# Linear attention ahead of two MoE layers: the low part of each turned chunk moves from VectorE to GpSimd, the squares are folded once, the scale goes into omega, and chunk 0 is prepared ahead of the loop

## The chip, the cores and the metric

The kernel runs on one core of a Trainium2 chip. The metric is the device time of one launch in microseconds. The engines are named as in the profile: PE is TensorE, ACT is ScalarE, DVE is VectorE, POOL is GpSimd, and SP is the engine whose queue issues the DMAs.

## The reference

Three stages run one behind the other, all in float32. Only the first is touched by the change.

```python
def _attn_ref(q, k, v, omega):            # q, k, v: (4, 8, 576, 64), omega: (128, 64)
    scale = 1.0 / np.sqrt(np.sqrt(D))
    q_s, k_s = (q * scale, k * scale)
    def phi(x):
        proj = np.einsum('bhsd,md->bhsm', x, omega)
        sq = np.sum(x * x, axis=-1, keepdims=True) / 2.0
        h = proj - sq
        h = h - np.max(h, axis=-1, keepdims=True)
        return np.exp(h) / np.sqrt(m)
    q_p, k_p = (phi(q_s), phi(k_s))
    kv = np.einsum('bhsm,bhsd->bhmd', k_p, v)
    z = np.sum(k_p, axis=2)
    num = np.einsum('bhsm,bhmd->bhsd', q_p, kv)
    den = np.einsum('bhsm,bhm->bhs', q_p, z)[..., None] + 1e-06
    return num / den
```

Behind it come a gated feed-forward layer (2304 tokens, 512 to 1536 to 512) and a second layer of 8 experts with a gate that is balanced by 8 rounds of row and column sums.

## The kernel before

Matmuls keep float32 precision by splitting each operand into a high part (a rounded copy, made by ACT) and a low part (the operand less the high part), and adding three products: high by high, high by low, low by high. For a chunk of the attention these are lines L529, L530 and L531; L531 is the one that reads the low part of the chunk.

The attention cuts q and k into 36 chunks of 128 partitions by 512 columns: a tail of k, then k and q in turn, with the tails of k and q in between. From chunk 1 on the odd chunks are k and the even ones q, but for the tails (17 is a tail of k, 18 and 35 are tails of q). Each chunk is loaded twice, turned (`xt`) for the matmul and as it is (`x`) for the sum of squares.

The work is a software pipeline that is written out by hand. A loop runs over steps; in each step the list `ORDER` is gone through from first to last, and an entry `(name, k)` does stage `name` for chunk `step - k`. Each engine does its instructions in the order in which they are written, so `ORDER` fixes every engine's queue. The stages that matter here, with the lines of the profile:

- `s0` (one chunk ahead, k = -1): POOL squares `x` (L492) into the one buffer `xx`, folds 64 columns to 32 (L494) and 32 to 16 (L495).
- `s0r` (k = 0): DVE sums the rest to `ssq` (L501). `s0n` (k = 0): POOL scales it to `nsq` (L507).
- `s1a` (k = 1): ACT makes the high part of the turned chunk (L477). `s1b` (k = 1): DVE makes its low part (L481).
- `s2p` (k = 2): PE projects the chunk, 12 matmuls (L529 to L531). `s2m`: DVE takes the maxima of both halves (L536). `s2b`, `s2c`: DVE makes `hm` (L540) and the bias `bi` (L544). `s2x`: ACT does the exponentials with that bias (L551, 8 instructions).
- `s3` to `s5` (k = 3 to 8): sums of keys by values (L566, L567) for a k chunk; transposes, numerator, division and the way back (L571, L584, L600, L612 to L622, L632, L643, L648) for a q chunk. On ACT two of these stand ahead of `s1a` in every even step, the copy L584 and the cast L643; in odd steps there is none.
- `pump`: twice in a step, one piece of the conversion of the next layer's float64 weights (L195 to L213 and L181), on ACT, DVE or POOL.

In ACT's queue the cast of chunk n (`s1a`, in step n + 1) stands behind the exponentials of chunk n - 2 (step n). From the last steps on the first MoE layer fills PE, which stays full to the end of the kernel. The chunk `x` has three buffers and the turned one four.

Of the kernel before, what the change touches and what calls it, by code (L numbers as in the profile page):

```python
# [11 lines left out]
F32 = mybir.dt.float32  # L12
F32R = mybir.dt.float32r
AF = mybir.ActivationFunctionType
ALU = mybir.AluOpType
# [5 lines left out]
P = 128  # L21
# [13 lines left out]
SCALE = float(D) ** -0.25  # L35
# [11 lines left out]
def f(ap):  # L47
    return ap.bitcast(F32)


class Kernel:
    def __init__(self, tc, x, v, vt, omega, wg, wv, wo, w2g, w1, w2, out):
# [7 lines left out]

    ORDER = [("s3a0", 4), ("s0r", 0), ("s5a", 8), ("s2p0", 2), ("s1a", 1), ("s2m0", 2), ("s2p1", 2), ("s40", 5),
# [3 lines left out]
    RINGS = dict(tr3=(0, 3), tr5=(4, 5, 6, 7, 2, 1), pr=(4, 5, 6, 7, 2, 1), nu=(4, 5, 6,  # L67
                 7, 2, 1), a=(0, 1, 2, 3), b=(4, 5, 6, 7))

# [329 lines left out]
    def attention(self, m1):  # L399
        tc, nc = self.tc, self.nc  # L400
        if True:
# [8 lines left out]
            sm = af  # L410
# [6 lines left out]
            om2 = t3[:, 0, 0:M]  # L417
            bdh, bdl = t6[:, 0], t6[:, 1]
# [19 lines left out]
            NCH = len(chunks)  # L438
            st = [dict() for _ in chunks]
# [4 lines left out]
            def load(i):  # L444
                side, bp, hp, j = chunks[i]
                c = st[i]
                n = 8 if hp is None else 2 * hp + j
                k = turn("x", 3)
                xt = c["xt"] = xts[turn("xt", 4)]
                c["x"] = t0[:, k].rearrange("p (a d) -> p a d", d=D)  # L450
                for w, t in ((1, xt), (0, t0[:, k])):
                    nc.sync.dma_start(t, self.x["qk".index(side), w, bp, n])
                c["idx"] = (lambda a, h: 2 * a + h) if hp is None else (lambda a, h: 4 * h + a)

            def loadv(i):
                side, bp, hp, j = chunks[i]
                c = st[i]
                if side == "q":
                    return
                if hp is None:  # L460
                    c["vz"] = vzts[2 * bp:2 * bp + 2]
                    for j in range(2):
                        nc.sync.dma_start(c["vz"][j].rearrange("p a d -> p (a d)"), self.vt[bp, j])
                else:
                    z = c["vz"] = vz[nvz[0] % NVZ]
                    nvz[0] += 1
                    nc.sync.dma_start(z.rearrange("p a d -> p (a d)"), self.v[bp, 2 * hp + j])
# [10 lines left out]

            def s1b(i):
                c = st[i]  # L480
                nc.vector.tensor_tensor(c["xl"], c["tr"], f(c["xh"]), op=ALU.subtract)  # L481

            def s0(i):
                c = st[i]
                sqv = c["x"]
                if i < self.EARLY:
                    c["xx"] = t2[:, i].rearrange("p (a d) -> p a d", d=D)
                    c["ssq"] = sm.tile([P, 8], F32, tag="ssq", name=f"ssq{i}", bufs=4)
                    nc.scalar.activation(c["xx"], sqv, AF.Square)
                    return  # L490
                xx = t0[:, 3].rearrange("p (a d) -> p a d", d=D)
                nc.gpsimd.tensor_tensor(xx, sqv, sqv, op=ALU.mult)  # L492
                ssq = sm.tile([P, 8], F32, tag="ssq", name=f"ssq{i}", bufs=4)
                nc.gpsimd.tensor_tensor(xx[:, :, 0:32], xx[:, :, 0:32], xx[:, :, 32:64], op=ALU.add)  # L494
                nc.gpsimd.tensor_tensor(xx[:, :, 0:16], xx[:, :, 0:16], xx[:, :, 16:32], op=ALU.add)  # L495
                c["xx"], c["ssq"] = xx, ssq

            def s0r(i):
                c = st[i]
                xx = c["xx"] if i < self.EARLY else c["xx"][:, :, 0:16]  # L500
                nc.vector.tensor_reduce(c["ssq"], xx, axis=AX.X, op=ALU.add)  # L501

            def s0n(i):
                c = st[i]
                nsq = sm.tile([P, 8], F32, tag="nsq", name=f"nsq{i}", bufs=4)
                eng = nc.vector if i < self.EARLY else nc.gpsimd
                eng.tensor_scalar(nsq, c["ssq"], -SCALE * SCALE / 2, None, op0=ALU.mult)  # L507
                c["nsq"] = nsq

            def s2(i):  # L510
                side, bp, hp, j = chunks[i]
# [25 lines left out]

            def s2b(i):
                c = st[i]
                nc.vector.scalar_tensor_tensor(c["hm"], c["mx"], SCALE, c["nsq"], op0=ALU.mult, op1=ALU.add)  # L540

            def s2c(i):
                c = st[i]
                nc.vector.scalar_tensor_tensor(c["bi"], c["hm"], -1.0, c["nsq"], op0=ALU.mult, op1=ALU.add)  # L544

            def s2x(i, u):
                c = st[i]
                e, bi = c["e"], c["bi"]
                for a in range(4 * u, 4 * u + 4):
                    pr = c["pr"][a // 4].rearrange("p w (h m) -> p (w h) m", m=M)  # L550
                    nc.scalar.activation(e[:, a, :], pr[:, a % 4, :], AF.Exp, bias=bi[:, a:a + 1], scale=SCALE)  # L551

            def s3(i, h):
                side, bp, hp, j = chunks[i]
# [94 lines left out]
                st[i] = None  # L649

            pump = lambda i: self.attn_pump()
            fns = dict(s0=s0, s0r=s0r, s0n=s0n, s1=s1, s1a=s1a, s1b=s1b, s2=s2, s2b=s2b, s2c=s2c, s4r=s4r, s5=s5, s5a=s5a, s5b=s5b, pump=pump)
            halves = dict(s2p=s2p, s2m=s2m, s2x=s2x, s3=s3, s3a=s3a, s4=s4, s4d=s4d, s4n=s4n)

            def stage(n):
                if n in fns:
                    return fns[n]
                g, h = halves[n[:-1]], int(n[-1])
                return lambda i: g(i, h)

            order = [(stage(n), k) for n, k in self.ORDER]
            nc.sync.dma_start(om2, self.omega)
            load(0)
            load(1)
            for h in range(2):
                r = slice(h * D, (h + 1) * D)
                nc.scalar.copy(bdh[r, h, :], om2[r])
                nc.vector.tensor_tensor(bdl[r, h, :], om2[r], f(bdh[r, h, :]), op=ALU.subtract)
            s0(0)
            for step in range(NCH + 8):  # L670
                if step == NCH + 2:
                    self.rings = self.DRAIN
                if step + 2 < NCH:
                    load(step + 2)
                if step == 0:
                    loadv(0)
                if step + 1 < NCH:
                    loadv(step + 1)
                for fn, n in order:
                    i = step - n  # L680
                    if 0 <= i < NCH:
                        fn(i)
                self.attn_hook(step)
                if step >= NCH + 2:
                    next(m1)
# [868 lines left out]
```

## Time and profile before

| | |
|---|---|
| time, median of 3 runs | 2113.62 us (2111.9 to 2114.81) |
| span of the profiled execution | 2111.6 us; its own time is not listed apart |
| PE busy over the span | 2061.5 us (98%) |
| DVE, POOL, ACT busy over the span | 66%, 50%, 39% |

The span runs from the first to the last instruction; what the median has over it (2.0 us) lies around it. Busy shares are over the whole span, and the attention is only about its first 180 us, so the stretch of the attention has to be looked at by itself.

### The profile page before, as it was taken

What the parts mean: (1) busy time and instruction counts of PE and PEld (TensorE: products, weight loads), DVE (VectorE), ACT (ScalarE), POOL (GpSimd) and SP (SyncE); (2) the same over time, 40 slices, a digit from 0 to 9 for tenths busy, and PEclk for the clock granted to TensorE, in tenths of its full rate; (3) what the DMA queues carried; (4) which work ended last, traced back from release to release, by engine and by line L of the source; (5) the groups of instructions that cost most, each with busy time, mean ns of one, the idle gap of its engine ahead of it and who ended that gap; (6) DMA issues with size and microseconds to landing.
All of it is one profiled execution on the core that took longest, in us unless ns stands there. A gap on an engine that the chain in (4) does not pass through costs nothing.

```text
span 2111.6 us, 32611 instructions
## 1 busy us (share of the span) xinstructions
PE 2061.5 (98%) x11836; PEld 1991.5 (94%) x11836; DVE 1400.0 (66%) x2321; ACT 825.3 (39%) x1843; POOL 1053.2 (50%) x1047
## 2 busy tenths in 40 slices
PE   7999999999999999999999999999999999999998
PEld 6889999999998889998898999999999999999998
DVE  6996678778655645444544666666687666666666
ACT  6776433333335444433433432323323432323322
POOL 6783656656533455545642544343454444343443
PEclk9999999999999999999999999999999999999999
DMA  6452556555424665666668777777877877787884
GB/s 212 166 165 66 176 165 200 179 165 187 133 80 175 235 236 209 253 254 251 230 254 301 242 259 257 260 255 263 278 259 268 273 258 258 258 257 255 244 269 152
DMA packets 238129, 467.76 MB, mean 222 GB/s; under 512 B 20272, under 2 KB 110096, under 8 KB 233872
## 3 DMA queue, kind: packets, MB, share of 16 engines
q1 hardware_dynamic: 237968, 465.68, 65.7%
q8 instruction: 93, 1.52, 0.3%
q14 instruction: 68, 0.56, 0.1%
HBM read 340.25 MB, written 125.35 MB: 220 GB/s over the span
## 4 chain that ended last, share of the span: by engine, by line
PE 89%; DVE 7%; POOL 1%; issue 1%; DMA 1%; ACT 1%; SPq 0%; DVEq 0%; ACTq 0%; POOLq 0%
PE bank L1079 12%; PE pair L1416 7%; PE pair L1418 7%; PE pair L1417 7%; PE bank L1325 7%; PE bank L1327 7%; PE bank L1326 7%; PE bank L723 5%; PE bank L724 5%; PE bank L725 5%; PE bank L1020 4%; PE bank L1022 3%; PE bank L1021 3%; PE bank L755 2%; PE bank L757 2%; PE bank L756 2%
## 5 line engine op out<-in xcount | busy, mean ns | idle before, releaser
L1428 DVE TENSOR_TENSOR sums<-pair,sums 128x768 f32<-128x768 f32 x209 | 198.7, 951 | 44.4 <-PE pair L1418 44.3
L1325 PE MATMUL bank<-xh,ar 128*128 128x384 f32 x564 | 188.7, 335 | 2.4 <-ACT mt L1358 2.0
L1327 PE MATMUL bank<-xh,ar 128*128 128x384 f32 x564 | 188.5, 334 | 0.0
L1326 PE MATMUL bank<-xl,ar 128*128 128x384 f32 x564 | 188.4, 334 | 0.0
L1095 DVE SCALAR_TENSOR_TENSOR ac<-bank,mt,ac 128x512 f32<-128x512 f32 x84 | 63.0, 750 | 129.9 <-PE bank L1079 128.1
L1416 PE MATMUL pair<-xh,ar 128*128 128x384 f32 x344 | 115.3, 335 | 0.0
L1417 PE MATMUL pair<-xl,ar 128*128 128x384 f32 x344 | 114.9, 334 | 0.0
L1418 PE MATMUL pair<-xh,ar 128*128 128x384 f32 x344 | 114.9, 334 | 0.0
L1325 PEld LDWEIGHTS bank<-xh,ar 128*128 128x128 f32 x564 | 105.9, 188 | 3.4 <-ACT mt L1358 2.7
L1326 PEld LDWEIGHTS bank<-xl,ar 128*128 128x128 f32 x564 | 105.9, 188 | 0.0
L1327 PEld LDWEIGHTS bank<-xh,ar 128*128 128x128 f32 x564 | 105.9, 188 | 0.0
L737 ACT CAST ar<-mt 128x384 fp32r<-128x384 f32 x72 | 37.0, 514 | 171.9 <-DVE mt L734 171.9
L723 PE MATMUL bank<-xh,ar 128*128 128x384 f32 x288 | 96.7, 336 | 0.0
L725 PE MATMUL bank<-xh,ar 128*128 128x384 f32 x288 | 96.2, 334 | 0.0
L725 PE MATMUL bank<-xh,ar1b 128*128 128x384 f32 x288 | 96.2, 334 | 0.0
L724 PE MATMUL bank<-xl,ar 128*128 128x384 f32 x288 | 96.2, 334 | 0.0
L724 PE MATMUL bank<-xl,ar1b 128*128 128x384 f32 x288 | 96.2, 334 | 0.0
L723 PE MATMUL bank<-xh,ar1b 128*128 128x384 f32 x288 | 96.2, 334 | 0.0
L551 ACT ACTIVATE at<-bank,bi 128x128 f32<-128x128 f32 x288 | 78.2, 383 | 42.5 <-DVE bi L544 33.2
L1020 PE MATMUL bank<-xh,ar 128*128 128x384 f32 x264 | 89.4, 338 | 3.2 <-DVE st L1054 2.5
L1022 PE MATMUL bank<-xh,ar 128*128 128x384 f32 x264 | 88.7, 336 | 2.8 <-DVE ar L265 2.7
L1021 PE MATMUL bank<-xl,ar 128*128 128x384 f32 x264 | 88.3, 335 | 0.0
(382 smaller groups left out, 6919.9 us busy)
## 6 DMA issues: line engine op xcount, KB each, us to landing
ar<-w2forms SPq DMA_DIRECT2D x144, 512.0 KB, 4.5
ar<-w1forms SPq DMA_DIRECT2D x141, 512.0 KB, 4.9
ar1b<-w1forms SPq DMA_DIRECT2D x62, 512.0 KB, 4.9
ar1b<-w2forms SPq DMA_DIRECT2D x61, 512.0 KB, 4.5
w2forms<-ar SPq DMA_DIRECT2D x224, 128.0 KB, 4.1
w1forms<-ar SPq DMA_DIRECT2D x22, 1280.0 KB, 7.1
sumsraw<-in_w_dram SPq DMA_DIRECT2D x32, 512.0 KB, 4.5
w2forms<-sumsraw SPq DMA_DIRECT2D x128, 128.0 KB, 2.7
```

What stands on the lines that cost most here:

```text
L723: nc.tensor.matmul(t, hi[:, c, fs], self.xh[:, c, cs], start=(c == 0), stop=False)
L724: nc.tensor.matmul(t, hi[:, c, fs], self.xl[:, c, cs], start=False, stop=False)
L725: nc.tensor.matmul(t, lo[:, c, fs], self.xh[:, c, cs], start=False, stop=(c == KC - 1))
L1020: nc.tensor.matmul(g, ah[:, c, :], bh[:, c, :], start=(first and c == 0), stop=False, skip_group_check=not first)
L1079: nc.tensor.matmul(y, a, w[:, fi % 2, ds], start=(first and x == 0 and k == 0 and fi == fis[0]), stop=(last and x == 1 and fi == fis[-1]))
L1325: nc.tensor.matmul(g, w[:, 0, d], bh[:, d, :], start=bool(first and d == 0), stop=False, skip_group_check=not first)
L1326: nc.tensor.matmul(g, w[:, 0, d], bl[:, d, :], start=False, stop=False, skip_group_check=not first)
L1327: nc.tensor.matmul(g, w[:, 1, d], bh[:, d, :], start=False, stop=(d == 1), skip_group_check=not first)
L1416: nc.tensor.matmul(y, w[:, k, 0, ds], h, start=(k == 0), stop=False)
L1417: nc.tensor.matmul(y, w[:, k, 0, ds], l, start=False, stop=False)
L1418: nc.tensor.matmul(y, w[:, k, 1, ds], h, start=False, stop=(k == 1))
L1428: v.tensor_tensor(a[n], pair, a[n], op=ALU.add)
```

## The change

The low part of a chunk (`s1b`) goes from DVE to POOL for every chunk but chunk 0, and its entry in `ORDER` moves up to stand right behind `s1a`, ahead of `s0`. `s0` loses its second fold, so `s0r` reads 32 columns in place of 16. `s0n` is gone: `hm` and `bi` are each made in one step from `ssq`. The scale is put into omega once, ahead of the loop. `s1`, `s1a`, `s1b` and `s0` of chunk 0 (`EARLY` is 1) are done ahead of the loop.

```diff
-    ORDER = [("s3a0", 4), ("s0r", 0), ("s5a", 8), ("s2p0", 2), ("s1a", 1), ("s2m0", 2), ("s2p1", 2), ("s40", 5),
-             ("s2m1", 2), ("s2b", 2), ("s2c", 2), ("s3a1", 4), ("s0", -1), ("s1b", 1), ("pump", 3), ("s2", 1),
+    ORDER = [("s3a0", 4), ("s0r", 0), ("s5a", 8), ("s2p0", 2), ("s1a", 1), ("s1b", 1), ("s2m0", 2), ("s2p1", 2),
+             ("s40", 5), ("s2m1", 2), ("s2b", 2), ("s2c", 2), ("s3a1", 4), ("s0", -1), ("pump", 3), ("s2", 1),
...
             def s1b(i):
                 c = st[i]
-                nc.vector.tensor_tensor(c["xl"], c["tr"], f(c["xh"]), op=ALU.subtract)
+                eng = nc.vector if i < self.EARLY else nc.gpsimd
+                eng.tensor_tensor(c["xl"], c["tr"], f(c["xh"]), op=ALU.subtract)
...
                 nc.gpsimd.tensor_tensor(xx[:, :, 0:32], xx[:, :, 0:32], xx[:, :, 32:64], op=ALU.add)
-                nc.gpsimd.tensor_tensor(xx[:, :, 0:16], xx[:, :, 0:16], xx[:, :, 16:32], op=ALU.add)
...
-                xx = c["xx"] if i < self.EARLY else c["xx"][:, :, 0:16]
+                xx = c["xx"] if i < self.EARLY else c["xx"][:, :, 0:32]
                 nc.vector.tensor_reduce(c["ssq"], xx, axis=AX.X, op=ALU.add)
-
-            def s0n(i):
...
-                nc.vector.scalar_tensor_tensor(c["hm"], c["mx"], SCALE, c["nsq"], op0=ALU.mult, op1=ALU.add)
+                nc.vector.scalar_tensor_tensor(c["hm"], c["ssq"], -SCALE * SCALE / 2, c["mx"], op0=ALU.mult, op1=ALU.add)
...
-                nc.vector.scalar_tensor_tensor(c["bi"], c["hm"], -1.0, c["nsq"], op0=ALU.mult, op1=ALU.add)
+                nc.vector.scalar_tensor_tensor(c["bi"], c["ssq"], -SCALE * SCALE / 2, c["hm"], op0=ALU.mult, op1=ALU.subtract)
...
-                    nc.scalar.activation(e[:, a, :], pr[:, a % 4, :], AF.Exp, bias=bi[:, a:a + 1], scale=SCALE)
+                    nc.scalar.activation(e[:, a, :], pr[:, a % 4, :], AF.Exp, bias=bi[:, a:a + 1])
...
-                nc.scalar.copy(bdh[r, h, :], om2[r])
-                nc.vector.tensor_tensor(bdl[r, h, :], om2[r], f(bdh[r, h, :]), op=ALU.subtract)
-            s0(0)
+                nc.scalar.activation(bdh[r, h, :], om2[r], AF.Copy, scale=SCALE)
+                nc.vector.scalar_tensor_tensor(bdl[r, h, :], om2[r], SCALE, f(bdh[r, h, :]), op0=ALU.mult, op1=ALU.subtract)
+            for fn in (s1, s1a, s1b, s0):
+                for i in range(self.EARLY):
+                    fn(i)
...
-                    if 0 <= i < NCH:
+                    if 0 <= i < NCH and not (i < self.EARLY and fn in (s1, s1a, s1b, s0)):
                         fn(i)
```

The line numbers of the changed kernel are a few lower (L481 becomes L482, L492 L493, L494 L495, L540 L533, L544 L537). On POOL, in the middle of the attention, one step stood like this before (`at_96` holds `x` and the squares; L210 and L213 are pieces of the weight conversion):

```order
L210 TENSOR_TENSOR m1raw_0_1_183<-m1raw_0_1_183 128x512
L492 TENSOR_TENSOR at_96<-at_96 128x512
L494 TENSOR_TENSOR at_96<-at_96 128x8x32
L495 TENSOR_TENSOR at_96<-at_96 128x8x16
L507 TENSOR_SCALAR nsq_733<-ssq_644 128x8
L213 TENSOR_TENSOR cv<-cv,m1raw_0_1_183 128x512
```

The same place in the changed kernel (`ar_62` holds the high and low parts of the turned chunks):

```order
L210 TENSOR_TENSOR m1raw_0_1_174<-m1raw_0_1_174 128x512
L482 TENSOR_TENSOR ar_62<-turned,ar_62 128x512
L493 TENSOR_TENSOR at_96<-at_96 128x512
L495 TENSOR_TENSOR at_96<-at_96 128x8x32
L213 TENSOR_TENSOR cv<-cv,m1raw_0_1_174 128x512
```

The low part now stands in POOL's queue ahead of the squares of the chunk two further on, and the second fold and `nsq` are gone. On DVE one step stood like this before:

```order
L501 TENSOR_REDUCE ssq_297<-at_96 128x8
L536 TENSOR_REDUCE mx_302<-bank_79 128x4
L536 TENSOR_REDUCE mx_302<-bank_71 128x4
L540 SCALAR_TENSOR_TENSOR hm_303<-mx_302,nsq_268 128x8
L544 SCALAR_TENSOR_TENSOR bi_304<-hm_303,nsq_268 128x8
L481 TENSOR_TENSOR ar_62<-turned,ar_62 128x512
L206 TENSOR_SCALAR m1raw_0_0_181<-cv 128x512
```

The same step on DVE in the changed kernel:

```order
L501 TENSOR_REDUCE ssq_283<-at_96 128x8
L529 TENSOR_REDUCE mx_286<-bank_79 128x4
L529 TENSOR_REDUCE mx_286<-bank_71 128x4
L533 SCALAR_TENSOR_TENSOR hm_287<-ssq_198,mx_286 128x8
L537 SCALAR_TENSOR_TENSOR bi_288<-ssq_198,hm_287 128x8
L206 TENSOR_SCALAR m1raw_0_0_172<-cv 128x512
```

The low part is gone from DVE's queue; the sum L501 still stands ahead of the two maxima. The order on ACT and on PE is the same in the loop.

## Rows read from the trace of the kernel before

**Rows 1.** The page: busy time, share of the span and instructions of each engine.

```profile
PE 2061.5 (98%) x11836; PEld 1991.5 (94%) x11836; DVE 1400.0 (66%) x2321; ACT 825.3 (39%) x1843; POOL 1053.2 (50%) x1047
```

**Rows 2.** Busy us (instructions) of each engine by stage, clock, DMA share, GB/s.

```profile
43.80:165.90 122.10, 112.09 (x934) 106.89 (x932) 116.19 (x261) 95.52 (x294) 92.99 (x118) 0.97 0.50 164
180.00:200.00 20.00, 20.00 (x150) 19.62 (x150) 13.14 (x26) 8.85 (x19) 9.60 (x11) 1.00 0.08 25
```

**Rows 3.** The chain that ended last, 100 to 110: start, us, what.

```profile
105.49 1.23 DVE ar L481
...
106.77 0.38 PE bank L531
```

**Rows 4.** Groups by line, 43.8 to 165.9: busy us, mean ns, idle before.

```profile
L481 DVE TENSOR_TENSOR ar<-turned,ar 128x512 fp32r<-128x512 f32 x27 | 26.6, 985 | 0.0
L492 POOL TENSOR_TENSOR at<-at 128x512 f32<-128x512 f32 x25 | 26.0, 1039 | 20.0 <-DVE ssq L501 19.9
L507 POOL TENSOR_SCALAR nsq<-ssq 128x8 f32<-128x8 f32 x27 | 16.5, 610 | 3.0 <-DVE ssq L501 0.8
L495 POOL TENSOR_TENSOR at<-at 128x128 f32<-128x128 f32 x26 | 14.1, 542 | 2.0
L181 POOL TENSOR_TENSOR ar<-cv,ar 128x512 fp32r<-128x512 f32 x5 | 6.4, 1288 | 0.4
L206 DVE TENSOR_SCALAR m1raw<-cv 128x512 int32<-128x512 int32 x5 | 2.1, 416 | 0.0
```

**Rows 5.** DVE's timeline, steps 21 and 22: start us, us, what.

```profile
98.31 0.27 DVE L501 TENSOR_REDUCE ssq<-at 128x8 f32<-128x128 f32 x1
...
99.81 0.72 DVE L540 SCALAR_TENSOR_TENSOR hm<-mx,nsq 128x8 f32<-128x8 f32 x1
100.56 0.17 DVE L544 SCALAR_TENSOR_TENSOR bi<-hm,nsq 128x8 f32<-128x8 f32 x1
100.64 0.96 DVE L481 TENSOR_TENSOR ar<-turned,ar 128x512 fp32r<-128x512 f32 x1
```

**Rows 6.** POOL's timeline there.

```profile
98.66 1.04 POOL L492 TENSOR_TENSOR at<-at 128x512 f32<-128x512 f32 x1 [1.44 <-DVE ssq L501]
99.78 0.72 POOL L494 TENSOR_TENSOR at<-at 128x256 f32<-128x256 f32 x1
100.58 0.47 POOL L495 TENSOR_TENSOR at<-at 128x128 f32<-128x128 f32 x1
```

**Rows 7.** ACT's timeline, from the exponentials of step 21 to the cast in step 23.

```profile
100.84 2.17 ACT L551 ACTIVATE at<-bank,bi 128x128 f32<-128x128 f32 x8 [2.07 <-DVE bi L544]
102.85 0.64 ACT L584 COPY at<-bank 128x512 f32<-128x512 f32 x1
103.31 0.66 ACT L643 CAST xh<-bank 128x512 fp32r<-128x512 f32 x1
103.79 0.70 ACT L477 CAST ar<-turned 128x512 fp32r<-128x512 f32 x1
...
105.69 2.17 ACT L551 ACTIVATE at<-bank,bi 128x128 f32<-128x128 f32 x8 [0.71 <-DVE bi L544]
107.70 0.67 ACT L477 CAST ar<-turned 128x512 fp32r<-128x512 f32 x1
```

**Rows 8.** The bias of chunk 7 and that of chunk 33, on DVE's timeline.

```profile
43.65 0.17 DVE L544 SCALAR_TENSOR_TENSOR bi<-hm,nsq 128x8 f32<-128x8 f32 x1
...
165.74 0.17 DVE L544 SCALAR_TENSOR_TENSOR bi<-hm,nsq 128x8 f32<-128x8 f32 x1
```

**Rows 9.** The head, all engines' timeline: chunk 0's sum, chunk 1's squares, `hm` and bias.

```profile
5.69 0.69 DVE L501 TENSOR_REDUCE ssq<-at 128x8 f32<-128x512 f32 x1 [0.82 <-ACT at L489]
6.57 1.04 POOL L492 TENSOR_TENSOR at<-at 128x512 f32<-128x512 f32 x1 [4.84 <-DMA at<-in_x_dram]
...
18.72 0.17 DVE L540 SCALAR_TENSOR_TENSOR hm<-mx,nsq 128x8 f32<-128x8 f32 x1
...
18.93 0.17 DVE L544 SCALAR_TENSOR_TENSOR bi<-hm,nsq 128x8 f32<-128x8 f32 x1
```

More of the change, by code (lines that the diff above doesn't have):

```diff
@@ L499, in s0r @@
                 c = st[i]
-                xx = c["xx"] if i < self.EARLY else c["xx"][:, :, 0:16]
+                xx = c["xx"] if i < self.EARLY else c["xx"][:, :, 0:32]
                 nc.vector.tensor_reduce(c["ssq"], xx, axis=AX.X, op=ALU.add)
-            def s0n(i):
[L504 to L508, printed above, removed]
             def s2(i):
@@ L651, in attention @@
             pump = lambda i: self.attn_pump()
-            fns = dict(s0=s0, s0r=s0r, s0n=s0n, s1=s1, s1a=s1a, s1b=s1b, s2=s2, s2b=s2b, s2c=s2c, s4r=s4r, s5=s5, s5a=s5a, s5b=s5b, pump=pump)
+            fns = dict(s0=s0, s0r=s0r, s1=s1, s1a=s1a, s1b=s1b, s2=s2, s2b=s2b, s2c=s2c, s4r=s4r, s5=s5, s5a=s5a, s5b=s5b, pump=pump)
             halves = dict(s2p=s2p, s2m=s2m, s2x=s2x, s3=s3, s3a=s3a, s4=s4, s4d=s4d, s4n=s4n)
```

4 rows, old and new, of the table ORDER are left out of this document.

## The prediction, made before the changed kernel ran

> **What bounds the kernel now.** I look at the whole first, then at the stage that the change touches. By the page PE is busy 98% of the span [rows 1], and behind the attention it is full: 20.00 of 20.00 us [rows 2]. So what the attention takes more or less goes into the time in full, and nothing after it can be won. In the steady part of the attention, 43.8 to 165.9 us, PE is busy 112.09 of 122.10 us and DVE 116.19; ACT (95.52) and POOL (92.99) have room [rows 2]. The chain that ended last runs there along DVE, and at its end PE waits for the low part, DVE's L481 [rows 3]. So DVE bounds this stage, with PE close behind.
>
> The pace comes from the bias of chunk 7, which starts at 43.65, and that of chunk 33 at 165.74 [rows 8]: 13 pairs of steps (one k chunk, one q chunk) in 122.1 us, 9.39 us a pair.
>
> DVE and POOL also hold each other up. `hm` is a tiny operation that takes 0.17 us when nothing is in its way [rows 9]. At 99.81 it took 0.72 and ended at 100.53, when POOL's fold L494 ended (99.78 + 0.72 = 100.50) [rows 5, 6]. The low part that began at 100.64 during L495 ended at 101.60, which is 0.55 behind L495's end at 101.05 [rows 5, 6]. So an operation of DVE with two inputs in SBUF starts its work when the running operation of POOL ends.
>
> **The change, part by part.** Off DVE goes L481, 0.985 us a step [rows 4]. The sum L501 reads 256 elements in place of 128: 0.27 us for 128 [rows 5] and 0.69 for 512 [rows 9] give, on a line, 0.41, so +0.14. `hm` and `bi` stay two operations of the same shape. Omega's scale stands ahead of the loop in instructions that were there already, and the exponentials lose only a constant: both are set at nothing, since no instruction comes in; the bound is the few tenths that two operations ahead of the first squares could take. By load alone DVE falls by about 1.7 us a pair and is no longer the bound.
>
> Off POOL go L495 (0.542) and L507 (0.610) [rows 4]; on it comes the low part. Its price there is that of the same kind of operation, L181: a 512-column subtraction from float32 into the rounded format, 1.288 us [rows 4]. The load of POOL hardly changes, and POOL is idle 20.0 us ahead of L492 alone [rows 4]. By load nothing bounds but PE.
>
> But the order makes a new ring. On POOL the low part of chunk n now stands ahead of the squares of chunk n + 2, and it waits for ACT's cast of chunk n, which stands behind the exponentials of chunk n - 2. Behind the squares waits DVE's sum of chunk n + 2, and DVE's queue has behind it the maxima, `hm` and bias of chunk n, and these release the exponentials of chunk n. What was beside the ring before (POOL's squares waited for DVE's last sum alone [rows 4]) is now in it. Once around is one pair of steps. I add it up for the even steps, where ACT has two more instructions ahead of the cast: From the bias's end (100.56 + 0.17) to the exponentials at 100.84 it is 0.11 [rows 5, 7]. From the exponentials to the end of the cast L477 (103.79 + 0.70) it is 3.65 [rows 7]. The handover to POOL is set at 0.08, the gap between two of its own operations (98.66 + 1.04 to 99.78) [rows 6]. The low part is 1.29 [rows 4] and a gap of 0.08. Squares and fold, 98.66 to 100.50, are 1.84 [rows 6]. The handover to DVE is 0.08 again. From the sum to `hm`, 98.31 to 99.81, it is 1.50 [rows 5], and 0.14 more for the wider sum. `hm` and bias, not held up, are 18.72 to 19.10, 0.38 [rows 9].
>
> That is 9.15 us a pair. `hm` is held up, though. Count from the end of the fold: `hm` is ready at 0.08 + 1.64 = 1.72. POOL has its next low part (odd steps, cast ready early, since there ACT needs only 107.70 + 0.67 - 105.69 = 2.68 us [rows 7]) at 0.08 to 1.37 and squares at 1.45 to 2.49. So `hm` meets squares, ends at 2.51 in place of 1.89, and the ring is 9.77. If a piece of the weight conversion stands between, `hm` meets the low part instead and ends at about the same time. So GpSimd's work hinders the bias as before, and 9.77 is slower than 9.39.
>
> To this I add 0.25 for the weight conversion on DVE and ACT, which can hold up POOL's chain or the cast. Per stage there are five lines of DVE with five operations each, some 25, half of them in even steps, so one a pair at 0.416 [rows 4]; the bounds are 0 and about 0.6 (that, and ACT's share), and I take less than half since some of it falls where POOL waits anyway. So 10.02 a pair, 0.63 more than now, and over 13 pairs +8.2 us.
>
> The head: chunk 0's low part comes ahead of the loop, so PE's first projection starts sooner, but the first maxima stand on DVE behind the sum of chunk 2, that is, behind two rounds of squares that start at 6.57 as before, when chunk 1 has landed [rows 9]. From there: sum of chunk 1 at 8.5, squares and fold of chunk 2 to 10.8, low part of chunk 1 to 12.2, squares and fold of chunk 3 to 14.1, `hm` of chunk 1 at 15.8, bias end 16.2, where it was 19.10 [rows 9]: 2.9 us earlier. Up to chunk 7 the ring is shorter by the casts and copies that come in later (0.48 and 0.46, the steps between ACT's instructions [rows 7]): 8.8, 9.3 and 9.3 us. 16.2 + 27.4 = 43.6, where the bias ended at 43.82. So the head's gain is used up by chunk 7: -0.2.
>
> The loads of turned chunks now wait for POOL in place of DVE. They are issued four chunks ahead, and I set this at nothing; the cover is the better part of a pair, and if it were gone, the squares would come late by what is missing.
>
> Sum: +8.2 - 0.2 = +8.0 on a span of 2111.6, that is 2119.6, and 2121.6 with the 2.0 us that the median has over it.
>
> One rule speaks against the change and gives its main term another price. The row has 1.288 us for such a low part on POOL [rows 4], where DVE needed 0.55 us from the moment that it had its way [rows 5, 6]. The Trainium skill, page GPSIMD Engine Reference, section 3.1 (Elementwise — side-by-side cycle accounting), has a two-input operation of 2048 elements at 4497 ns on GpSimd against 2293 ns on VectorE, about twice. A quarter of the first is 1.12 us, an estimate by that section of the Trainium skill; with it the ring would be 0.17 shorter a pair and the time 2.2 us less, 2119.4. I go by the row.
>
> **The rivals.**
>
> *`hm` slips in ahead of the squares.* The margin is 0.27 us (1.72 against 1.45). If the odd low part starts 0.3 later, because its cast is late, `hm` runs first and the ring is 9.15 to 9.4: -3.1 to 0 over 13 pairs, and -0.7 at the head. About 2111.5. Against it: ACT's odd cast needs 0.97 us less than the even one (3.65 less 2.68), so there POOL and not the cast should come last.
>
> *PE becomes the bound.* If the ring is shorter than its parts add up to, PE's own 112.09 us in 122.10 is the floor: -10.0, and the head's 2.9 are kept: 2100.7. This is what the loads alone say, and it decides as soon as the ring falls below 8.6 us. Against it: four engines' queues in a fixed order, each with a row.
>
> *The ring is longer still.* The granted clock was 0.97 in this stage [rows 2]; with more waits of PE it can fall oftener, and the weight conversion can take its full 0.6. That gives +0.35 a pair and a few us of clock: 2129.
>
> **How the numbers follow.** The forecast has 0.55, `hm` ahead of the squares 0.20, PE as the bound 0.15, the longer ring 0.10. The predicted time is the first's, 2121.6; its own range, with 9.77 to 10.4 a pair, is 2117 to 2127. The range of 8 in 10 takes in the second and leaves out most of the third and the fourth: 2107 to 2129. A measurement of this kernel can tell about 0.2% (4.2 us) from no change. Faster than 2109.4: the third and a little of the second, 0.18. Within 0.2%: most of the second and the low end of the first, 0.29. Slower: 0.53.
>
> **What would show it.** In the changed profile POOL's low part should take about 1.29 us and wait for ACT's cast in even steps; DVE's sum should wait for POOL's fold in most steps; DVE should fall below 85% busy in the stage; and the bias should come every 10.0 us a pair. The sum without waits, and PE above 95% busy, would show the third case. Wrong price of the handovers, or `hm` at 0.17 us, would make the prediction wrong.

## The result, and the profile after

The changed kernel takes 2130.56 us (median of 4 runs, 2128.39 to 2133.01) against 2114.22 us (4 runs, 2111.9 to 2116.24) for the kernel before on the same chip: ratio 1.007, 95% interval 1.0055 to 1.0084. It is slower, by about 16 us where 8 were forecast, and 1.6 us beyond the range. The profiled execution has a span of 2131.2 us and a time of 2133.01.

The changed kernel's page, busy time of each engine over the span, against [rows 1]:

```profile
PE 2077.4 (97%) x11836; PEld 2004.7 (94%) x11836; DVE 1394.8 (65%) x2285; ACT 824.5 (39%) x1843; POOL 1061.7 (50%) x1012
```

The windows of [rows 2], changed kernel (busy us of PE, PEld, DVE, ACT, POOL with instructions, then granted clock, DMA share, GB/s):

```profile
43.80:165.90 122.10, 108.22 (x828) 101.65 (x827) 100.38 (x214) 85.51 (x264) 87.96 (x83) 0.92 0.47 148
180.00:200.00 20.00, 19.16 (x153) 18.13 (x152) 10.31 (x30) 13.14 (x38) 2.80 (x3) 1.00 0.00 1
```

DVE fell from 116.19 us to 100.38, but PE, ACT and POOL fell too: in the same 122 us fewer instructions ran on every engine. Nothing is busier, and all wait more. At 180 us the attention is not over yet.

DVE's timeline of the changed kernel at the bias of chunks 7 and 33 (start us, us, what), against [rows 8]:

```profile
45.08 1.27 DVE L533 SCALAR_TENSOR_TENSOR hm<-ssq,mx 128x8 f32<-128x8 f32 x1
46.39 0.96 DVE L537 SCALAR_TENSOR_TENSOR bi<-ssq,hm 128x8 f32<-128x8 f32 x1
...
182.15 0.17 DVE L537 SCALAR_TENSOR_TENSOR bi<-ssq,hm 128x8 f32<-128x8 f32 x1
```

The bias of chunk 7 ends at 47.35, where it was 43.82 and 43.6 was forecast; that of chunk 33 ends at 182.32, where it was 165.91. The 13 pairs between take 10.38 us each (9.39 before, 10.02 forecast). The difference at chunk 33, 16.4 us, is as large as that of the medians (16.3). The two profiled spans lie another 3.2 us apart, which arises behind the attention: from the bias of chunk 33 to the end it takes 1945.7 us before, 1948.9 in the changed kernel, and 1946.3 to 1950.2 in the other profiled executions of this document. So the attention's time goes into the total to within some 5 us, and that the two differences agree so closely is in part luck.

The waits of the changed kernel from 47.4 to 182.3 us (in total, times, longest):

```profile
POOL ar L482 <- ACT ar L477: 34.4, 18, 4.1
ACT at L544 <- DVE bi L537: 23.1, 12, 4.3
DVE ssq L501 <- POOL at L495: 21.5, 13, 2.9
...
PE bank L522 <- ACT at L544: 10.2, 10, 1.5
...
PE bank L524 <- POOL ar L482: 1.5, 2, 0.8
```

The first could not be before, and the third was one wait of 0.6 us in the window of [rows 2]: POOL waits for ACT's cast, and DVE's sum waits for POOL's fold. PE waits for the exponentials to free its banks; the last line says that it hardly ever waits for the low part itself. The chain that ended last, which ran along DVE in [rows 3], runs along POOL in the changed kernel (start, us, what):

```profile
99.07 1.27 POOL ar L482
100.35 1.00 POOL at L493
101.34 0.04 issue
101.43 0.86 POOL at L495
102.29 2.87 issue
105.20 1.28 POOL ar L482
```

The 2.87 us of "issue" are POOL's wait for ACT's cast, which this view does not follow further; the timelines below do.

One turn of the ring can be walked through three timelines of the changed kernel. DVE's, against [rows 5]:

```profile
98.57 0.42 DVE L501 TENSOR_REDUCE ssq<-at 128x8 f32<-128x256 f32 x1 [2.54 <-POOL at L495]
98.91 1.28 DVE L529 TENSOR_REDUCE mx<-bank 128x4 f32<-128x512 f32 x2
100.22 0.17 DVE L533 SCALAR_TENSOR_TENSOR hm<-ssq,mx 128x8 f32<-128x8 f32 x1
100.42 0.94 DVE L537 SCALAR_TENSOR_TENSOR bi<-ssq,hm 128x8 f32<-128x8 f32 x1
...
107.35 0.92 DVE L204 SCALAR_TENSOR_TENSOR cv<-m1raw,cv 128x512 int32<-128x512 int32 x1
108.90 0.42 DVE L501 TENSOR_REDUCE ssq<-at 128x8 f32<-128x256 f32 x1 [0.62 <-POOL at L495]
...
110.75 0.91 DVE L537 SCALAR_TENSOR_TENSOR bi<-ssq,hm 128x8 f32<-128x8 f32 x1
```

ACT's, against [rows 7]:

```profile
101.46 2.18 ACT L544 ACTIVATE at<-bank,bi 128x128 f32<-128x128 f32 x8 [2.28 <-DVE bi L537]
103.48 0.64 ACT L577 COPY at<-bank 128x512 f32<-128x512 f32 x1
103.94 0.66 ACT L636 CAST xh<-bank 128x512 fp32r<-128x512 f32 x1
104.42 0.70 ACT L477 CAST ar<-turned 128x512 fp32r<-128x512 f32 x1
```

POOL's, against [rows 6]:

```profile
99.07 1.27 POOL L482 TENSOR_TENSOR ar<-turned,ar 128x512 fp32r<-128x512 f32 x1 [0.54 <-ACT ar L477]
100.30 1.04 POOL L493 TENSOR_TENSOR at<-at 128x512 f32<-128x512 f32 x1
...
105.20 1.27 POOL L482 TENSOR_TENSOR ar<-turned,ar 128x512 fp32r<-128x512 f32 x1 [2.91 <-ACT ar L477]
106.42 1.30 POOL L493 TENSOR_TENSOR at<-at 128x512 f32<-128x512 f32 x1
107.80 1.06 POOL L495 TENSOR_TENSOR at<-at 128x256 f32<-128x256 f32 x1
```

Sum at 98.57, bias from 100.42 to 101.36, exponentials at 101.46, the cast's end at 105.12, the low part at 105.20, the fold's end at 108.86, the next sum at 108.90, the next bias's end at 111.66. That is 10.30 us from bias to bias with no slack in any link. And the bias, an operation of 0.17 us, takes 0.94: it ends 0.02 behind the squares L493, which run from 100.30 to 101.34.

### The profile page after: what moved, and what is told of

It is laid out like the page before. It is cut to its first block, busy times and chain, and to the rows that moved or that the text cites. A ratio compares the mean times of both kernels' runs of the same rounds, so it can differ in the third digit from the quotient of the medians.

```text
span 2131.2 us, 32584 instructions
## 1 busy us (share of the span) xinstructions
PE 2077.4 (97%) x11836; PEld 2004.7 (94%) x11836; DVE 1394.8 (65%) x2285; ACT 824.5 (39%) x1843; POOL 1061.7 (50%) x1012
## 4 chain that ended last, share of the span: by engine, by line
PE 88%; POOL 4%; DVE 3%; issue 2%; ACT 1%; DMA 1%; POOLq 0%; DVEq 0%; ACTq 0%
PE bank L1074 12%; PE pair L1411 7%; PE pair L1412 7%; PE pair L1413 7%; PE bank L1320 7%; PE bank L1321 7%; PE bank L1322 7%; PE bank L718 5%; PE bank L719 5%; PE bank L720 5%; PE bank L1015 4%; PE bank L1017 3%; PE bank L1016 3%; PE bank L750 2%; PE bank L752 2%; PE bank L751 2%
## 5 line engine op out<-in xcount | busy, mean ns | idle before, releaser
L544 ACT ACTIVATE at<-bank,bi 128x128 f32<-128x128 f32 x288 | 79.2, 408 | 60.2 <-DVE bi L537 33.6
```

## The experiments

Every kernel was timed beside the kernel before; a ratio under 1 is faster than that kernel. The changed kernel stands at 1.007.

**Is the ring the cause?** The first experiment puts the low part back behind the squares on POOL, and changes nothing else.

```diff
-    ... ("s1a", 1), ("s1b", 1), ("s2m0", 2), ... ("s0", -1), ("pump", 3), ...
+    ... ("s1a", 1), ("s2m0", 2), ... ("s0", -1), ("s1b", 1), ("pump", 3), ...
```

> The changed kernel with one entry of ORDER moved: the low part on GpSimd stands behind the squares of the step, not ahead of them. All engines do the same work. Ring theory (the low part ahead of the squares closes a ring of exponentials, cast, low part, squares, sum, bias): the ring is open, the bias comes every 8.7 to 9.2 us a pair in place of 10.38, and the time is 2100 to 2112, faster than before the change. Rival (GpSimd's operations are dearer and hold up hm and bias wherever they stand): the pace stays at 10 or more and the time at 2125 or more.

Measured: 2118.36 us, ratio 1.0015 (1.0002 to 1.0028), 9.63 us a pair. The ring opens and gives back about 12 us, but the kernel is no faster than before, where 2100 to 2112 was expected. What holds the open order was a second question, taken up below.

The second keeps the order on POOL and issues ACT's cast ahead of the exponentials, the copy and the other cast, which shortens the ring at another place.

```diff
-    ORDER = [("s3a0", 4), ("s0r", 0), ("s5a", 8), ("s2p0", 2), ("s1a", 1), ("s1b", 1), ...
+    ORDER = [("s1a", 1), ("s3a0", 4), ("s0r", 0), ("s5a", 8), ("s2p0", 2), ("s1b", 1), ...
```

> The changed kernel with one entry of ORDER moved: ScalarE makes the cast of the turned chunk as the first of a step, ahead of the copy of the transposes and the cast of the turned output. Ring theory: 0.94 a pair leave the ring (0.46 and 0.48 in even steps), so 9.4 to 9.7 us a pair and 2115 to 2122. Rival (GpSimd's operations are dearer wherever they stand, the order does not matter): no change, 2127 or more.

Measured: 2119.87 us, ratio 1.0016 (1.0002 to 1.0029), 9.79 us a pair. The time is in the range that the ring gave: ACT's cast is in it, and POOL's load, which is unchanged here, is not the cause. The pace fell by 0.59 where 0.94 was expected. From exponentials to cast's end it is 2.78 us in place of 3.74, as it should be, but in some turns DVE's sum now starts 0.8 to 1.4 us behind the fold: the shorter ring no longer holds every turn.

The third lengthens the ring by the second fold that the change took out.

```diff
+                nc.gpsimd.tensor_tensor(xx[:, :, 0:16], xx[:, :, 0:16], xx[:, :, 16:32], op=ALU.add)
...
-                xx = c["xx"] if i < self.EARLY else c["xx"][:, :, 0:32]
+                xx = c["xx"] if i < self.EARLY else c["xx"][:, :, 0:16]
```

> The changed kernel with the second fold on GpSimd put back, so that VectorE sums 16 columns again. Ring theory: 0.54 and a gap of 0.08 come into the ring and 0.14 of the sum leaves it, so about 0.5 a pair slower over 13 pairs and a little at the head: 2135 to 2141. Rival (VectorE's load sets the pace): VectorE is relieved of 0.14 a step, and the time is 2131 or less.

Measured: 2138.0 us, ratio 1.0095 (1.0068 to 1.0123), 10.63 us a pair. The time is in the range that the ring gave, and POOL's squares and folds take 2.49 us a turn in place of 2.03. The pace of the profiled execution rose by 0.25 only, where about 0.5 was expected.

The fourth gives the squares two buffers in turn, so that they need not wait for the last sum.

```diff
-                xx = t0[:, 3].rearrange("p (a d) -> p a d", d=D)
+                xx = (t0[:, 3], bx[:, 3584:4096])[i % 2].rearrange("p (a d) -> p a d", d=D)
```

> The changed kernel (low part ahead of the squares on GpSimd) with the same two buffers in turn for the squares. If the ring runs through ScalarE's cast and GpSimd's low part, and not through the buffer, nothing moves: 10.3 to 10.5 us a pair, 2127 to 2133 us. If the single buffer is what holds the changed kernel: 9.9 a pair or less, 2120 us or less.

Measured: 2128.85 us, ratio 1.0057 (1.0037 to 1.0077), 10.35 us a pair. Nothing moves beyond the noise: the buffer is not in the ring.

The fifth takes `hm` and the bias out of the ring. The squares cancel in `h` less its maximum, so the bias can come from the projections alone: omega is scaled by the negative of the scale, and the minimum of a projection is the bias.

```diff
...
-                nc.vector.reduce_max(c["mx"][:, 4 * u:4 * u + 4], ...)
+                nc.vector.tensor_reduce(c["bi"][:, 4 * u:4 * u + 4], ..., op=ALU.min)
...
-                    nc.scalar.activation(e[:, a, :], pr[:, a % 4, :], AF.Exp, bias=bi[:, a:a + 1])
+                    nc.scalar.activation(e[:, a, :], pr[:, a % 4, :], AF.Exp, bias=bi[:, a:a + 1], scale=-1.0)
```

> The changed kernel's order on GpSimd, but the bias comes out of one minimum over the projections with omega scaled by the negative of SCALE, so hm and bi are gone; squares, fold and sum are still made and nobody reads the sum. If the ring over the sum, hm and bi sets the pace: 1.34 us from the start of hm to the end of the bias leaves it, and the sum with it; about 9.0 us a pair, 2110 to 2118 us. If hm and bi held up by GpSimd are not on the path: 2126 us or more.

Measured: 2100.65 us, ratio 0.9926 (0.99 to 0.9952), 8.58 us a pair (9.0 expected), and below the range of 2110 to 2118. Its windows over those 13 pairs, and its waits there:

```profile
39.30:150.80 111.50, 106.60 (x933) 104.24 (x932) 82.92 (x182) 95.14 (x295) 97.68 (x93) 0.98 0.57 179
```

```profile
DVE ssq L501 <- POOL at L495: 23.8, 18, 2.6
...
POOL ar L482 <- ACT ar L477: 11.4, 9, 1.8
```

The sum still waits for the fold 18 times, so the ring is still closed, only shorter, and PE is 96% busy (106.60 of 111.50). The size was off in the main because the exponentials of a chunk's first half now start on the first half of the bias, 0.51 us ahead of the bias's end (means by step are in the table below).

**Do the other parts of the change cost anything?** The open order of the first experiment, with the low part on VectorE again and all else as in the changed kernel:

```diff
-                eng = nc.vector if i < self.EARLY else nc.gpsimd
+                eng = nc.vector
```

> The changed kernel with the low part back on VectorE at its old place; one fold, hm and bias from ssq, scaled omega and the prepared chunk 0 stay. Ring theory: VectorE bounds as before, with a wider sum (0.14 a step) and less of GpSimd in its way: 9.3 to 9.7 us a pair, 2110 to 2119. Rival (one of the other parts costs the time, such as hm and bias made from ssq, or the preparation ahead of the loop): 2122 or more.

Measured: 2118.98 us, ratio 1.0013 (1.0000 to 1.0025), 9.86 us a pair. In the total, one fold less, the scale in omega, the two steps for the bias and chunk 0 ahead of the loop come to next to nothing together. It is made up of two parts, though: the bias of chunk 7 ends 3.5 us earlier than before the change (40.28 against 43.82), and the pairs behind it are 0.46 us slower each (9.3 to 9.7 were expected). Which of the parts costs that was not tested. With the squares first, the engine of the low part makes no difference to the time (2118.36 on POOL).

Chunk 0's preparation back inside the loop, all else as changed:

```diff
-            for fn in (s1, s1a, s1b, s0):
-                for i in range(self.EARLY):
-                    fn(i)
+            s0(0)
...
-                    if 0 <= i < NCH and not (i < self.EARLY and fn in (s1, s1a, s1b, s0)):
+                    if 0 <= i < NCH:
```

> The changed kernel with the preparation of chunk 0 back inside the loop. The preparation ahead of the loop brought the first bias from 19.1 to 16.05 us; if that stays with the rest of the attention: 2131 to 2134 us, 1 to 3 us over the changed kernel. If the ring's first turns take it back: no difference, 2129 to 2131 us or less.

Measured: 2129.99 us, ratio 1.0066 (1.0045 to 1.0087). No difference. The bias of chunk 1 ends at 16.32 us without the preparation, 16.05 with it and 19.10 before [rows 9], so most of the gain at chunk 1 is not the preparation's; what it comes from stays open.

**What holds the open order at 9.63?** My second theory was that `hm` and the bias held up by POOL are its price. In the kernel of the first experiment, DVE and POOL show (timelines):

```profile
67.41 0.72 DVE L533 SCALAR_TENSOR_TENSOR hm<-ssq,mx 128x8 f32<-128x8 f32 x1
68.16 1.19 DVE L537 SCALAR_TENSOR_TENSOR bi<-ssq,hm 128x8 f32<-128x8 f32 x1
```

```profile
67.38 0.73 POOL L495 TENSOR_TENSOR at<-at 128x256 f32<-128x256 f32 x1
68.06 1.27 POOL L482 TENSOR_TENSOR ar<-turned,ar 128x512 fp32r<-128x512 f32 x1
```

So the open order got the bias by minimum as well (the edit of the fifth experiment on top of the first's; squares and sum are made and not read):

> The kernel of e1_squares_first (low part on GpSimd behind the squares), with omega scaled by the negative scale, so that one minimum over the projections is the bias itself: hm and bias as operations with two inputs are gone from VectorE. Squares and their sum are still made, though nothing reads them any more (they cancel in h less its maximum). Theory of the holds (what is left of the loss in e1_squares_first is that hm and bias each wait for a running operation of GpSimd, 1.35 us from hm's start to the bias's end where 0.37 would do): 8.6 to 9.0 us a pair in place of 9.63, 2104 to 2111. Rival (GpSimd's own load or PE's waits for the low part set the pace): 2115 or more.

Measured: 2118.23 us, ratio 1.0006 (0.9995 to 1.0016), 9.67 us a pair. The theory falls: without `hm` and the bias the open order is no faster. Its waits from 43 to 165 us and a stretch of POOL's timeline:

```profile
POOL at L493 <- DVE ssq L501: 24.0, 11, 4.8
...
PE bank L522 <- POOL ar L482: 13.8, 14, 3.6
```

```profile
105.00 1.04 POOL L493 TENSOR_TENSOR at<-at 128x512 f32<-128x512 f32 x1 [1.85 <-DVE ssq L501]
106.11 0.73 POOL L495 TENSOR_TENSOR at<-at 128x256 f32<-128x256 f32 x1
106.80 1.27 POOL L482 TENSOR_TENSOR ar<-turned,ar 128x512 fp32r<-128x512 f32 x1
```

Here the squares wait for the last sum to free the one buffer, the low part stands behind them, and PE waits for the low part. By this reading POOL's queue is a second ring in the open order, DVE's sum to squares to low part to PE to DVE. A second fold in it tests that, and the theory of the holds with it:

> The kernel of e1_squares_first with the second fold put back on GpSimd, between the first fold and the low part. GpSimd gets 0.54 us a step more to do. Theory of the holds (an operation of GpSimd that reads what the one ahead wrote leaves a gap of some 0.08 us, in which the bias slips through behind hm; an operation that does not leaves none, and the bias waits for the whole of it): the bias takes 0.17 us in most steps, the time is 2108 to 2117, not slower than e1_squares_first. Rival (GpSimd's load sets the pace there): slower, 2122 or more.

Measured: 2130.66 us, ratio 1.0058 (1.0040 to 1.0075): 9 us slower by the ratios (0.0043 of 2115), on the side of POOL's queue. The first half of the theory came true: 9 of 36 biases were held up, where it was 22 in the first experiment. So fewer holds gained nothing in the open order. The direct test is the first experiment with the two buffers of the fourth:

> The kernel of e1 (squares issued ahead of the low part on GpSimd) with two buffers in turn for the squares. In e1 the squares waited for the sum of the chunk before (23.9 us of waits in the attention) and the low part stood behind them. If that single buffer sets e1's pace of 9.63 us a pair: 8.7 to 9.2 a pair, 2104 to 2112 us, and the wait of the squares for the sum is gone. If it does not: 9.5 or more a pair, 2116 us or more.

Measured: 2114.45 us, ratio 0.9989 (0.9975 to 1.0002), 9.51 us a pair. The squares' wait for the sum is gone from the list, but the pace hardly moves (0.12 a pair where 0.4 to 0.9 was expected); the first wait of POOL is now another, the low part's for the cast (17.1 us, 2.2 in the first experiment). So the buffer was one holder of several, and what sets 9.51 stays open. The time lies between the two ranges that were given.

**A version that beats both.** Since the squares cancel, they can go altogether: no `x` load, squares, fold, sum, `hm` or bias step; the minimum is the bias. That leaves part of the reference's computation out (the squares, which cancel). First with the low part on VectorE, then with it on POOL behind the cast:

```diff
...
-                for w, t in ((1, xt), (0, t0[:, k])):
-                    nc.sync.dma_start(t, self.x["qk".index(side), w, bp, n])
+                nc.sync.dma_start(xt, self.x["qk".index(side), 1, bp, n])
...
-            def s0(i):
...
-            def s0r(i):
...
-            def s2b(i):
...
-            def s2c(i):
...
```

> No squares at all: the bias is the minimum of the negated projections, since the squares cancel in h less its maximum; the loads of the unturned chunks, the squares, folds, sums, hm and bias are gone; the low part is on VectorE at its old place. PE's own work is the floor: 8.6 to 8.9 us a pair and an earlier first bias, 2096 to 2105. Rival (release of the banks by the exponentials, or the weight conversion, sets the pace): 2109 or more.

> The same without squares, with the low part on GpSimd behind the pumped conversion's place of the step. GpSimd has only the low part and the weight conversion to do, so no ring and no hold of hm or bias is left: 2096 to 2105, within 3 us of the version with the low part on VectorE. Rival (the move of the low part to GpSimd costs by itself, through its longer 1.29 us ahead of PE): 4 us or more slower than that version.

Measured: 2089.28 us, ratio 0.9869 (0.9849 to 0.9889) on VectorE; 2088.44 us, ratio 0.986 (0.9838 to 0.9881) on POOL: both below the range of 2096 to 2105, at 8.03 and 7.99 us a pair. The window from 40 to 140 us with the low part on POOL:

```profile
40.00:140.00 100.00, 99.15 (x900) 98.50 (x900) 66.92 (x147) 91.81 (x284) 50.13 (x40) 1.00 0.42 130
```

PE is full, and the low part's engine does not matter: 1.27 us on POOL costs nothing when no other work of POOL stands on the way to the bias. Some 72 matmuls a pair keep PE busy for 7.9 us here and did so for 8.6 before [rows 2], so the 8.6 that was put as PE's floor was not one.

## Why the prediction was wrong, point by point

The ring is there as forecast, but one step of it was put too short, and the forecast loss is about half of the measured one. The steps of the ring, in us, are means over the 13 odd chunks from 9 to 33, from the starts and ends in the timelines of DVE, POOL and ACT; the last two columns are the kernel with the preparation in the loop and that with the bias by minimum.

| step | forecast | changed | prep. in loop | by minimum |
|---|---|---|---|---|
| bias's end to exponentials | 0.11 | 0.11 | 0.11 | -0.51 |
| exponentials to cast's end | 3.65 | 3.74 | 3.74 | 3.75 |
| cast to low part | 0.08 | 0.08 | 0.08 | 0.42 |
| low part to squares | 1.37 | 1.23 | 1.23 | 1.23 |
| squares and fold | 1.84 | 2.03 | 2.04 | 2.04 |
| fold to sum | 0.08 | 0.03 | 0.03 | 0.03 |
| sum to `hm` (by minimum: sum to bias's end) | 1.64 | 1.80 | 1.65 | 1.62 |
| `hm` to bias's end | 1.00 | 1.34 | 1.28 | none |
| weight conversion, set apart | 0.25 | in the rows above | | |
| one turn, as measured | 10.02 | 10.38 | 10.16 | 8.58 |

- **What bounds the kernel before, and that the attention's time goes into the total in full:** right, to within the 5 us named above.
- **The load off DVE and the price on POOL:** right. L482 takes 1.273 us on POOL (26 of them), against 1.288 by the row and 1.12 by the estimate from the Trainium skill's GPSIMD Engine Reference, section 3.1; the measurement bears out the row. DVE is 82% busy in the window of [rows 2], below the 85% named.
- **The ring:** right, and shown by shortening it at two places (the cast first, the bias by minimum), opening it and lengthening it, each with the sign that it asks for, while the buffer that is not in it did nothing. POOL waited for the cast 18 times of 26, and DVE's sum for the fold 13 times, in half of the steps and not in most.
- **"`hm` is held up, though ... the ring is 9.77":** this step failed. I let `hm` wait for the squares (0.62) and the bias go free behind it in 0.17, as it did in [rows 5]. In the changed kernel the bias waits too. Of the 36, 20 took longer than 0.3 us, 1.06 on average; before, 2. Often `hm` comes at the very end of the low part and hardly waits, as at 100.22, and the bias meets the squares that began at 100.30; at chunk 7 both were held, 1.27 and 0.96. The term measured 1.34 in place of 1.00 in the steady part and 1.86 in the three pairs of the head: 13 x 0.34 + 3 x 0.86 = 7.0 of the 8.4 us that were missing at chunk 33. The other steps of the steady part nearly cancel: low part and fold are passed on 0.19 faster than forecast, and from sum to `hm` it is 0.16 longer, which the point on the clock takes up.
- **The head, "-0.2":** wrong, for the same reason in the main (2.6 of 3.9 us; the rest lies in the pair of chunk 3). The bias of chunk 1 came at 16.05 (16.2 forecast), but the next three pairs took 10.99, 9.91 and 10.40 us in place of 8.8, 9.3 and 9.3. The gain of 3 us was gone by chunk 5 and 3.5 us lost at chunk 7.
- **The weight conversion, 0.25:** about right, and most of it in POOL's chain. Squares and fold took 2.03 in place of 1.84: at 107.80 the fold took 1.06 us in place of 0.73, as DVE's L204, with two inputs in SBUF, had begun at 107.35, and at 106.42 the squares took 1.30 beside DVE's L201, another piece. From exponentials to cast it was 0.09 longer.
- **The clock:** not in the sum, only in the rival of a longer ring. The granted clock from 47.35 to 182.3 us was 0.92 on average, that is, about 16% of this stretch at 1.2 GHz, with PE busy 119.71 of 134.95 us. The kernel with the preparation in the loop had 0.99 from 47.7 to 179.8 and 10.16 us a pair. Turn by turn the two agree to 0.02 us, but for two: the turns of chunks 9 and 13 took 12.34 and 10.92 us in the changed kernel, 10.32 and 10.12 in the other. There the changed kernel's clock was at the lower level, 0.50, and PE was full (windows as above); the other's was at 1.00:

```profile
49.00:59.00 10.00, 10.00 (x49) 10.00 (x49) 8.18 (x15) 5.99 (x18) 7.14 (x7) 0.50 0.37 122
73.00:79.00 6.00, 6.00 (x29) 6.00 (x29) 4.10 (x8) 5.21 (x15) 4.40 (x5) 0.50 0.44 146
```

So the clock took some 0.2 of the 0.36 us a pair by which the pace of this execution missed the forecast; that this comes from the clock is read, not tested.

- **The rivals:** `hm` ahead of the squares came true in many steps, and helped nothing because the bias fell behind instead. PE as the bound was far off in this order, but comes as soon as `hm` and the bias's last step leave the ring (96% busy) or the squares are gone (99%). The longer ring is nearest to what happened: the clock that it named did fall, the weight conversion that it named did not grow, and the held bias was not in it.

## What to carry to other kernels

When an operation is moved to an idle engine, follow what then stands behind it in that engine's queue: here it put ScalarE's cast ahead of the squares and closed a ring through three engines (ScalarE, GpSimd, VectorE), though no engine was full. The link to shorten is the one that every turn passes: moving one entry of the order gave 12 us, taking two tiny operations out of the ring 30. Before a step is shared out among engines, ask whether it is needed; the squares cancelled.

## What the runs showed of the hardware

A DVE operation with two inputs in SBUF that is issued while a POOL operation runs waits until that one ends, however small it is: `hm` and the bias took 0.17 us alone and up to 1.3 beside POOL. All 35 that were held in the changed kernel (15 `hm`, 20 biases) ended 0.02 to 0.03 us behind the end of a POOL operation that had begun before them, and none waited for a second one. The maxima, which read PSUM, took 1.28 for two either way. The Trainium skill, page SBUF — State Buffer, section Who interferes with whom, says so: a DVE instruction with two SBUF inputs contends with a GpSimd instruction that reads SBUF, the lock is exclusive, and the order of issue decides who blocks. The traces agree in both directions: the bias at 100.42 took 0.94 behind the squares, the fold at 107.80 took 1.06 in place of 0.73 behind L204. Two inputs are not the only case in these traces: DVE's L199, 512 columns with one input in SBUF, took 0.41 to 0.43 us alone and 0.80 to 1.51 when it was issued while a POOL operation ran.

What I had not expected is that the next POOL operation decides over the second of two such DVE operations. The first, `hm`, gets through when the running POOL operation ends, and the bias is issued some 0.05 us after that end. Where POOL's next operation needs the result of the one before, it starts 0.08 us after that one's end (L492's end at 99.70, L494 at 99.78 in [rows 6]), and the bias of 0.17 us slips in ahead of it. Where L482, L493 or a piece of the weight conversion follows on a result that it does not need, it starts about 0.04 us before the one before has ended (68.06 against 67.38 + 0.73 = 68.11 in the first experiment), so the bias finds it running: at 68.16 it took 1.19 us and ended with that low part. The change replaced a dependent second fold by an independent low part or squares at this very place, and the second fold in the open order brought the held biases from 22 to 9. That the dependence itself sets the gap is not shown: L507 of the kernel before, an operation of 8 columns, did not need the result of L495 either and started 0.08 us behind its end.
